# Attention ahead of a gated layer: keys projected one pair of heads earlier, and two steps taken off TensorE

## The chip, the cores and the metric

The kernel runs on one core of one Trainium2 chip. The metric is the time of one execution in device microseconds; several executions are timed and their median is compared. A profiled execution has a span, from its first to its last instruction, and its own time, which is a little longer.

## The reference

What is computed, in short:

```python
batch, n_heads, seq, head_dim, n_features = 8, 8, 576, 64, 128

def phi(x):                                   # x: q or k, times 64 ** -0.25
    h = x @ omega.T - sum(x * x) / 2          # [.., seq, 128]
    return exp(h - max(h)) / sqrt(128)        # max over the 128 features of a token

q_p, k_p = phi(q_s), phi(k_s)
kv  = einsum('bhsm,bhsd->bhmd', k_p, v)
z   = k_p.sum(axis=2)                         # over the 576 tokens
num = einsum('bhsm,bhmd->bhsd', q_p, kv)
den = einsum('bhsm,bhm->bhs', q_p, z)[..., None] + 1e-06
x   = (num / den).transpose(0, 2, 1, 3).reshape(4608, 512)

out = ((x @ w_a) * (x @ w_b)) @ w_out         # 512 -> 1536 -> 512, float32
```

## The kernel before, in words

**Two parts.** The attention is done in 32 *pairs*: pair u = 4·b + hp holds heads 2·hp and 2·hp + 1 of batch b. The gated layer is done in *blocks* of the 512 first tokens of a batch (blocks 0 to 7), and block 8 takes the last 64 tokens of all batches. Blocks 0 and 1 multiply straight (`moe_block`: `pa`, `pb`, `o`); from block 2 on two blocks' halves are combined into seven products (sums of x: `Sa`, `Sb`; sums of weights: `t`, `bq`, which travel through DRAM; products `p`, their sums `c`; the product of both sides, `ghl`, times `wo`). Every fp32 product of the layer is three matmuls on a high and a low part, so each x, weight and product passes a CAST (mostly on ACT) and a subtraction (on DVE). While block b runs, the four pairs of batch b + 1 run between its matmuls.

**A pair.** `pair(u)` does the following, tiles named by u's batch and pair:

- `four` projects four chunks of 128 tokens at once, k on rows 0:64 of the array and q on rows 64:128 (`ppk`, `ppq`), copies them to `hk` and `hq`, and takes the maximum (DVE), the bias `sm`, and the exponential (ACT). Main chunks come twice, the last tokens of all four pairs of a batch once (`ht`).
- **z.** POOL adds the nine chunks of `hk` down to two rows of 128 features for each partition (`zs`). ACT and DVE split it into `zr`, and two matmuls with a matrix of ones sum it over the partitions and spread the sum to all of them: `pz`, copied by ACT to `zb`.
- **kv.** Ten matmuls sum k over the tokens (`pkv`, features along the free axis); ACT copies it (`k2`), PE transposes it (`pk`, with `ident`), ACT copies that (`kl`).
- **Division.** Ten DVE operations take each token's denominator (`dn`, from `hq` and `zb`), ACT scales the nine chunks of `hq` by its reciprocal.
- **Turn of q.** One DVE operation transposes `hq` by 32×32 blocks (`qd`); SP stores it to DRAM in four transfers (`qdr`) and loads it back over `hq`, features along the partitions. Pair 7 (`TURN`) and the pairs of batch 0 use nine transposes on PE instead (`pq`).
- **num.** `pm` = `kl` times the turned q; ACT and DVE make x's high and low part of it. The matmuls of `pm` wait in the list `pending` until the next pair's `pkv` takes them along; those of pairs 7 and 31 are issued by themselves.

Pairs 0 to 3 go another way (`tok_tail`).

**What sets the order.** All operations are recorded in a graph, with a planned cost for each engine, a priority, and a *margin*: planned nanoseconds that an operation stays behind the end of its inputs. `Graph.schedule` then walks over planned time and takes, over all engines, the operation that can start first; that is the order of each engine's instructions. A transfer is planned as its bytes at 330 per ns, one transfer behind another, plus 2000 ns:

```python
    def schedule(self, bw=330.0, dma_lat=2000):
...
                begin = max(s, dma_free)
                dma_free = begin + o.bytes / bw
                o.end = dma_free + dma_lat
```

Buffers come in rings of a given number of slots; an operation that needs a new one is placed when the slot's last user is done. SP issues nearly all transfers, in one queue; a transfer that waits for its data holds up those behind it. The first operation of a pair is kept behind a step of the block that runs (`GATES`, four numbers for the four pairs of a batch).

Of the kernel before, what the change touches and what calls it, by code (L numbers as in the profile page):

```python
# [17 lines left out]
P = 128  # L18
# [6 lines left out]
SM = 512  # L25
# [30 lines left out]
class Graph:  # L56
# [3 lines left out]
    def __init__(self):  # L60
        self.ops, self.rings, self.slots = [], {}, {}
# [172 lines left out]
def tile_attention_moe(ctx: ExitStack, tc: tile.TileContext, kqt, kqtt, kqn, kqnt, vx, omst, idn, wab, wout, out):  # L234
# [12 lines left out]
    for name, n in dict(X=2, Xw=0, nat=2, x2=0, v=2, h=CFG["H"], qd=1, kvz=1, sm=3, sq=3, ht=2, Xt=1, xl=0, xts=2, rd=2, x=4, xa=2, xf=2, Sa=2, Sb=2, st=0,  # L247
                        w=NF, u=NF, t=0, tst=0, wo=3, raw=2, a=2, c=0, bq=0, ghl=2, osb=0, ot=0, owr=0, og=0, ogf=0, oc=0, zs=1, z2=1, zb=1, k2=1, kl=2, dn=1, tails=1, zr=1,
# [6 lines left out]
    LATE = dict(wo=["h0", "h1"], ot=["X0", "X1", "h2", "qd0"], owr=["raw0", "raw1"], og=["nat0", "nat1", "ht0", "ht1"], ogf=["xf0", "xf1"],  # L255
# [34 lines left out]
    ones = fixed([P, P], F32R, "ones")  # L290
    junk = fixed([P, M], mybir.dt.bfloat16, "junk")
# [15 lines left out]
    g.op({"ACT": act(M)}, lambda e: nc.scalar.activation(ones.ap[:], om.ap[:], AF.Copy, scale=0.0, bias=1.0), r=[(om, None)], w=[(ones, None)], prio=3000)  # L307
# [134 lines left out]
    def four(nm, b, pri, x, xdep, dst, c0, sm, sq, al, deps, mg, more):  # L442
# [41 lines left out]
        for w in range(2):  # L484
            for c in some:
                g.op({"ACT": 392}, lambda e, c=c, w=w: nc.scalar.activation(  # L486
                    dst[w].ap[:, c], src[w](c), AF.Exp, scale=SC, bias=sm.ap[:, 2, w, c:c + 1]),
                    r=[(held[w][0] if len(held[w]) == 1 else (dst[w], c)), (sm, (c0, w))], w=[(dst[w], c)], prio=pri + 3 + w)
# [5 lines left out]
    def pair(u, gate):  # L494
# [59 lines left out]
        def zadd(eng, n, o, a, c, r, w, al=()):  # L554
            g.op({"POOL": pool2(n)}, lambda e: ENG[e].tensor_tensor(o(), a(), c(), op=ALU.add), r=r, w=w, alloc=list(al), prio=pri)  # L555
# [12 lines left out]
        g.op({"DVE": dve(2 * M)}, subber(lo, lambda: flat(zs), hi), r=[(zs, None), (zr, 0)], w=[(zr, 1)], prio=pri + 9)
        pz = g.buf("at", [P, 2 * M], F32, f"pz{nm}", more)

        def broadcast(e):
            nc.tensor.matmul(pz.ap[:], ones.ap[:], hi(), start=True, stop=False)
            nc.tensor.matmul(pz.ap[:], ones.ap[:], lo(), start=False, stop=True)
        g.op({"PE": mm(2, 2 * M)}, broadcast,
             r=[(zr, None), (ones, None)], w=[(pz, None)], alloc=[pz, zb], prio=pri + 10, margin=mg and mg + CFG["SUMS"])
        g.op({"ACT": act(2 * M)}, copier(lambda: zb.ap.rearrange("p j m -> p (j m)"), lambda: pz.ap[:]), r=[(pz, None)], w=[(zb, None)], prio=pri + 10)
# [19 lines left out]
        pk = g.buf("at", [P, 2, D], F32, f"pk{nm}", more)  # L596
        kl = g.buf("kl", [P, 2, D], F32, f"kl{nm}")
        g.op({"PE": 108}, lambda e: nc.tensor.transpose(pk.ap.rearrange("p j d -> p (j d)"), k2.ap[:], ident.ap[:]), r=[(k2, None), (ident, None)],
             w=[(pk, None)], alloc=[pk, kl], prio=pri + 5, margin=mg)
# [630 lines left out]
```

## Time and profile before

| | |
|---|---|
| runs shown (us) | 1075.25, 1071.83, 1072.91; median 1072.91 |
| profiled execution: own time, span | 1071.77, 1070.0 |
| granted TensorE clock | 1.00 |
| busy: PE, PE's weight loads, DVE, ACT, POOL | 1053.8, 928.8, 867.2, 591.1, 106.4 |
| idle time of PE | 16.2 |
| DMA | 305.61 MB in all, 286 GB/s; queue 1 (SP's) 303.55 MB, 82.8% of 16 engines' span |
| the chain that ended last | PE 82%, DVE 7%, ACT 5%, DMA 3% |

Times are in microseconds. Matmuls are pipelined, and an instruction's duration in the profile reaches into the next one's; from the start of one to the start of the next is shorter than the duration. A group of instructions has an engine, the tiles it writes and reads (`pz<-zr,ones`), a shape, a count, the busy time and the mean of one, and the engine's idle time just ahead of it with what ended most of it.

### The profile page before, as it was taken

How to read it: one execution, taken by the hardware profiler on the slowest of the kernel's cores; microseconds unless marked ns; L12 is line 12 of the kernel's file. 1: busy time of each engine (PE TensorE's matmuls, PEld its weight loads, DVE VectorE, ACT ScalarE, POOL GpSimd, SP SyncE). 2: the span in 40 equal slices, each digit the busy share in tenths (PEclk: the TensorE clock that was granted, in tenths of full speed). 3: DMA queues.
4: the chain of work that ended last, by engine and by line, in shares of the span. 5: the costliest groups of instructions: out<-in, count | busy, mean ns of one | idle time of the engine just before them, and what ended most of it. 6: DMA issues, size and time to landing. Idle time of an engine off the chain costs nothing.

```text
span 1070.0 us, 22015 instructions
## 1 busy us (share of the span) xinstructions
PE 1053.8 (98%) x7899; PEld 928.8 (87%) x7899; DVE 867.2 (81%) x2145; ACT 591.1 (55%) x1599; POOL 106.4 (10%) x176
## 2 busy tenths in 40 slices
PE   9999999999999999999999999999999999999997
PEld 7878777868788889888888988888888989999997
DVE  6999986989886788777886879778876777998766
ACT  7997767666764646554645566464645423333111
POOL 0021111111110101010111111010101000000000
PEclk9999999999999999999999999999999999999999
DMA  9877966797898888978888888988796799999991
GB/s 359 306 240 230 335 198 208 243 377 274 283 320 295 276 301 269 339 264 289 295 312 295 273 298 270 332 265 299 257 323 196 261 334 304 319 336 344 352 305 50
DMA packets 118270, 305.61 MB, mean 286 GB/s; under 512 B 16656, under 2 KB 35856, under 8 KB 118160
## 3 DMA queue, kind: packets, MB, share of 16 engines
q1 hardware_dynamic: 117296, 303.55, 82.8%
q8 instruction: 62, 1.02, 0.4%
q10 hardware_dynamic: 864, 0.66, 0.2%
q14 instruction: 48, 0.39, 0.1%
HBM read 249.43 MB, written 54.72 MB: 284 GB/s over the span
## 4 chain that ended last, share of the span: by engine, by line
PE 82%; DVE 7%; ACT 5%; DMA 3%; issue 1%; POOL 1%; SPq 0%; ACTq 0%; DVEq 0%
PE p L1047 34%; PE o L785 19%; PE ppk L452 5%; PE pb L956 5%; PE pa L956 5%; PE o_P L853 4%; PE pkv L588 3%; PE pm L647 2%; DMA td<-ts 1%; DVE c L1057 1%; ACT hq L619 1%; ACT hk L486 1%; DMA out_dram<-osb 1%; PE p L853 1%; PE pn L720 1%
## 5 line engine op out<-in xcount | busy, mean ns | idle before, releaser
L1057 DVE TENSOR_TENSOR c<-p,c 128x512 f32<-128x512 f32 (+1 forms) x336 | 207.7, 618 | 93.0 <-PE p L1047 86.7
L785 PE MATMUL o<-wo,ghl 128*128 128x512 f32 x1008 | 270.6, 397 | 0.3 <-DVE ghl L282 0.3
L785 PEld LDWEIGHTS o<-wo,ghl 128*128 128x128 f32 x1008 | 175.5, 188 | 32.0 <-DVE ghl L282 1.2
L1047 PE MATMUL p<-Sa,t 128*128 128x256 f32 x1008 | 144.6, 281 | 1.6 <-ACT c L274 1.6
L1047 PEld LDWEIGHTS p<-Sa,t 128*128 128x128 f32 x1008 | 133.1, 188 | 7.6 <-ACT c L274 2.4
L555 POOL TENSOR_TENSOR z<-hk 128x256 f32<-128x256 f32 x56 | 45.2, 807 | 690.3 <-ACT hk L486 488.9
L274 ACT COPY c<-p 128x256 f32<-128x256 f32 x84 | 31.1, 371 | 125.9 <-PE p L1047 72.7
L486 ACT ACTIVATE hk<-hk,sm 128x128 f32<-128x128 f32 x192 | 62.3, 392 | 46.7 <-DVE sm L482 38.7
L619 ACT ACTIVATE hq<-hq,dn 128x128 f32<-128x128 f32 x224 | 70.6, 392 | 26.6 <-DVE dn L615 24.9
L956 PE MATMUL pb<-x,wb 128*128 128x512 f32 x288 | 75.2, 401 | 0.0
L956 PE MATMUL pa<-x,wa 128*128 128x512 f32 x288 | 73.7, 398 | 0.9 <-DVE x L282 0.9
L1047 PE MATMUL p<-Sb,t 128*128 128x256 f32 x504 | 74.5, 283 | 0.0
L1047 PE MATMUL p<-Sb,bq 128*128 128x256 f32 x504 | 74.5, 283 | 0.0
L1047 PE MATMUL p<-x,t 128*128 128x256 f32 x504 | 73.7, 282 | 0.7 <-ACT oc L274 0.7
L1047 PEld LDWEIGHTS p<-x,t 128*128 128x128 f32 x504 | 69.1, 188 | 5.9 <-ACT oc L274 1.1
L452 PE MATMUL ppk<-om,X 64*128 64x128 f32 x512 | 73.9, 285 | 0.0
L452 PE MATMUL ppq<-om,X 64*128 64x128 f32 x512 | 73.4, 284 | 0.1
L452 PEld LDWEIGHTS ppk<-om,X 64*128 64x128 f32 x512 | 61.7, 187 | 13.5 <-issue 3.4
L1047 PE MATMUL p<-x,wb 128*128 128x256 f32 x504 | 71.2, 284 | 1.6 <-DVE c L1057 1.5
L609 DVE CUSTOM_DVE_ANT_0 junk<-hq,zb 128x128 bf16<-128x128 f32 x224 | 65.6, 293 | 8.6 <-ACT zb L274 6.5
L1047 PE MATMUL p<-x,wa 128*128 128x256 f32 x504 | 71.2, 286 | 1.0 <-DVE c L1057 0.9
L1047 PEld LDWEIGHTS p<-x,wb 128*128 128x128 f32 x504 | 65.9, 188 | 5.1 <-DVE c L1057 2.0
(185 smaller groups left out, 2027.5 us busy)
## 6 DMA issues: line engine op xcount, KB each, us to landing
t<-td SPq DMA_DIRECT2D x168, 512.0 KB, 5.6
wo<-wod SPq DMA_DIRECT2D x96, 512.0 KB, 5.8
bq<-bd SPq DMA_DIRECT2D x84, 256.0 KB, 5.6
X<-in_kqt_dram SPq DMA_DIRECT2D x31, 512.0 KB, 5.7
qdr<-qd SPq DMA_DIRECT2D x108, 144.0 KB, 4.3
hq<-qdr SPq DMA_DIRECT2D x27, 576.0 KB, 6.5
raw<-in_wab_dram SPq DMA_DIRECT2D x24, 512.0 KB, 6.2
td<-ts SPq DMA_DIRECT2D x24, 512.0 KB, 5.9
```

Source lines behind the costliest of these rows:

```text
L274: nc.scalar.copy(o(), i())
L452: nc.tensor.matmul(pps[w].ap[:, c * M:c * M + M], x()[rows, c * P:c * P + P], om.ap[rows], start=True, stop=True)
L486: g.op({"ACT": 392}, lambda e, c=c, w=w: nc.scalar.activation(dst[w].ap[:, c], src[w](c), AF.Exp, scale=SC, bias=sm.ap[:, 2, w, c:c + 1]), ...
L555: g.op({"POOL": pool2(n)}, lambda e: ENG[e].tensor_tensor(o(), a(), c(), op=ALU.add), r=r, w=w, alloc=list(al), prio=pri)
L588: nc.tensor.matmul(pkv.ap[D * j:D * j + D, 0:M], vb.ap[:, vc, 0:D], c(), start=(n == 0), stop=(n == 4))
L609: g.op({"DVE": 413}, lambda e, c=c, j=j, rr=rr, qc=qc: nc.vector.tensor_tensor_reduce(out=junk.ap[rr], in0=qc(), in1=zb.ap[rr, j], scale=1 ...
L619: g.op({"ACT": 392}, lambda e, c=c, src=src: nc.scalar.activation(hq.ap[:, c], src(), AF.Copy, scale=dn.ap[:, c:c + 1]), r=[sd, (dn, None) ...
L785: nc.tensor.matmul(po.ap[:], ghl.ap[:, gi, t * P:(t + 1) * P], wo.ap[:, wi], start=(n == 0 and i == 0), stop=(n == NF - 1 and i == 2))
L853: nc.tensor.matmul(pb.ap[:, t], A[0](ai)[:, t * P:(t + 1) * P], W[0](wi), start=begin and t == j == 0, stop=stop and t == 1 and j == 2)
L956: nc.tensor.matmul(pb.ap[:], wt.ap[:, wi, c], xs[c].at(xi), start=(c == 0 and i == 0), stop=(c == NC4 - 1 and i == 2))
L1047: nc.tensor.matmul(pb.ap[:, half], wcol(wi, c), xc(xi, c), start=n == 0, stop=n == 5)
L1057: g.op({"DVE": dve(n)}, lambda e: nc.vector.tensor_tensor(c4.ap[:, o], pb.ap[:, half], y(), op=ALU.add), r=[*((pb, k) for k in range(half. ...
```

## The change

From pair 4 on, `shifted` takes the place of `pair`. It changes these things:

1. **k runs a pair ahead of q.** `first_k` does the k side of pair 4 by itself. Then step u projects the k chunks of pair u + 1 together with the q chunks of pair u, so the number of projection groups is the same; the host lays the k chunks out anew. The ring `h` of three buffers becomes `hk` (one, eight chunks) and `hq` (two, ten chunks). The first pair of the next batch is now recorded ahead of every block, before only of blocks 2 to 6.
2. **z without PE.** POOL's adds stay. DVE transposes the two rows of 128 by 32×32 blocks, sums each block to one number per partition (`zq`), ACT brings the four groups of 32 partitions together (three small copies), DVE sums and transposes them (`zw`, `zx`). SP stores `zx` (1 KB, `zdr`) and loads it back to all partitions (`zb`, 128 KB). `zr`, `ones`, `pz` go.
3. **kv within q's transfers.** `k2` is transposed by DVE as a tenth chunk of `qd`, so the four stores have 160 KB instead of 144 and the load 640 instead of 576; ACT copies `kl` out of the loaded `hq`. `pk` goes. Pair 7 goes this way too, so its nine `pq` go.
4. **num two steps behind kv.** `pkv` of pair u + 1 takes along `pm` of pair u − 1. The last two `pm` are issued by themselves.
5. **Margins.** Behind the landings of `zb`, of the loaded `hq` and ahead of the first division and of `kl` there are planned margins that differ for batch 1, batch 2 and later ones (`ZD`, `ZB`, `BACK2`, `HQ`; `BACK` was 1500).

The core of the diff:

```diff
-CFG = dict(TW=(), ..., H=3, TURN=(7,), BACK=1500, ...)
+CFG = dict(ZS=800, ZB=(1500, 3000, 5000), ZD=(1500, 3000, 4500), HQ=(2500, 4000, 5000), BACK2=(1500, 2500, 4000), TW=(), ...)
...
-    for name, n in dict(X=2, ..., h=CFG["H"], qd=1, kvz=1, ..., ht=2, ..., zs=1, z2=1, zb=1, k2=1, kl=2, dn=1, tails=1, zr=1,
+    for name, n in dict(X=2, ..., hk=1, hq=2, qd=1, kvz=0, ..., ht=3, ..., zs=1, z2=1, zb=2, k2=2, kl=1, dn=1, tails=0, zq=2, zx=2,
...
+    def shifted(u, gate):
...
+            xb = load("X", [P, 8 * P], f"X{nm}", lambda: kqt[b, hp], early)
...
+                lead = [four(nm, b, pr + 10 * i, ..., [(hk, 0), (hq, 0)], 4 * i, sm, sq, ...)]
+            zbs[u + 1] = z_sums(u + 1, pr, hk, mg)
...
+            k2s[u + 1] = kv_burst(u + 1, pr + 40, hk, vb, 500)
...
+        divide(u, pr, hq, zbs[u])
+        qT = turn(u, pr, hq, k2s[u])
+        num(u, pr, hq, qT)
...
+    def mar(u, name):
+
+        return CFG[name][min(u // NHP, 3) - 1]
...
-        def broadcast(e):
-            nc.tensor.matmul(pz.ap[:], ones.ap[:], hi(), start=True, stop=False)
-            nc.tensor.matmul(pz.ap[:], ones.ap[:], lo(), start=False, stop=True)
...
+        def groups(e):
+            nc.vector.transpose(flat(z2), flat(zs))
+            nc.vector.tensor_reduce(zq.ap[:, 0], flat(z2).rearrange("p (c r) -> p c r", r=32), axis=X, op=ALU.add)
+        g.op({"DVE": 2 * dve(2 * M)}, groups, r=[(zs, None)], w=[(z2, None), (zq, 0)], alloc=[zq], prio=pri, margin=CFG["ZS"])
...
+            for i in range(1, 4):
+                nc.scalar.copy(zq.ap[0:32, i], zq.ap[32 * i:32 * i + 32, 0])
...
+            nc.vector.tensor_reduce(zw.ap[0:32, 0:8], zq.ap[0:32, 0:4].rearrange("p i c -> p c i"), axis=X, op=ALU.add)
+            nc.vector.transpose(zx.ap[0:32], zw.ap[0:32])
...
+        g.op({"SP": 330}, dma(lambda: zd, lambda: zx.ap[0:8]), ..., nbytes=32 * 8 * 4)
+        zload.append(g.op({"SP": 330}, dma(lambda: flat(zb), lambda: zd.rearrange("c r -> (c r)").partition_broadcast(P)), ..., margin=mar(u, "ZD")))
...
-        g.op({"PE": 108}, lambda e: nc.tensor.transpose(pk.ap.rearrange("p j d -> p (j d)"), k2.ap[:], ident.ap[:]), r=[(k2, None), (ident, None)],
-             w=[(pk, None)], alloc=[pk, kl], prio=pri + 5, margin=mg)
-        g.op({"ACT": act(2 * D)}, copier(lambda: kl.ap[:], lambda: pk.ap[:]), r=[(pk, None)], w=[(kl, None)], prio=pri)
...
+        g.op({"DVE": dve(M)}, lambda e: nc.vector.transpose(qd.ap[:, :, NCH], k2.ap.rearrange("p (j r) -> p j r", r=32)),
+             r=[(k2, None)], w=[(qd, 1)], prio=pr + 110)
...
+        g.op({"ACT": act(M)}, copier(lambda: kl.ap[:], lambda: view()[:, :, NCH]), r=[(hq, None)], w=[(kl, None)], alloc=[kl], prio=pr + 120, margin=mar(u, "HQ"))
...
-        ahead = 1 < b and b + 1 < B
-        if ahead:
+        if b + 1 < B:
             attention(b + 1, [0])
```

How this moves instructions is shown at three places. In the rows a tile's number behind its name tells one buffer's use from another; `x_3_3` is x of block 3 from its last pair, `t3_...` weights' sums of block 3.

**PE, where batch 4 begins.** Before, from the `pm` of pair 15 (`pm_3_3`, taken along by `pkv_4_0`) past `pz` and `pk` of pair 16:

```order
L647 MATMUL pm_3_3_4972<-hq_3_3_4323,kl_3_3_4744 64x512 x2
L649 MATMUL pkv_4_0_4970<-hq_3_3_4323,kl_3_3_4744 64x64 x2
L1047 MATMUL p1_3610<-x_2_2_3267,wb10_1679 128x256 x3
L1047 MATMUL p1_3610<-x_2_3_3563,wb10_1679 128x256 x3
L1047 MATMUL p1_3610<-Sa_2_0_3311,t2_510_4655 128x256 x3
L1047 MATMUL p1_3610<-Sa_2_1_3606,t2_510_4655 128x256 x3
L572 MATMUL pz_4_0_5017<-zr_4_0_4991,ones_68 128x256
L573 MATMUL pz_4_0_5017<-zr_4_0_4991,ones_68 128x256
L1047 MATMUL p0_3609<-Sa_2_0_3311,t2_510_4655 128x256 x3
L1047 MATMUL p0_3609<-Sa_2_1_3606,t2_510_4655 128x256 x3
L598 MATMUL pk_4_0_5030<-ident_66,k2_4_0_4971 128x128
```

Now, from the `pkv` of pair 17 on, which takes the same `pm_3_3` along:

```order
L696 MATMUL pkv_4_1_5169<-hk_4_1_4781,v_4_0_4453 64x128 x8
L696 MATMUL pkv_4_1_5169<-htk4_4567,v_4_0_4453 64x128 x2
L764 MATMUL pm_3_3_5171<-hq_3_3_4469,kl15_5156 64x512 x2
L766 MATMUL pkv_4_1_5169<-hq_3_3_4469,kl15_5156 64x64 x2
L903 MATMUL o2_1_4095<-wo2_8_4907,ghl2_8_5005 128x512 x3
L903 MATMUL o2_2_4125<-wo2_8_4907,ghl2_8_5005 128x512 x3
L903 MATMUL o2_3_4134<-wo2_8_4907,ghl2_8_5005 128x512 x3
L1165 MATMUL p1_3771<-x_3_2_4707,wa0_580 128x256 x3
L1165 MATMUL p1_3771<-x_3_3_5172,wa0_580 128x256 x3
```

No `pz` and no `pk` are left, and the first matmul that reads `x_3_3` stands 12 matmuls behind the burst with `pm_3_3`; before, 34 rows lay between them (one row is often three matmuls).

**ACT, at the same place.** Before, from the split of z to the copy of `pk`:

```order
L274 CAST zr_4_0_4991<-zs_4_0_4826 128x256
L274 CAST x_3_3_4973<-pm_3_3_4972 128x512
L274 COPY xts3_4103<-pkv_4_0_4970 128x64
L274 COPY k2_4_0_4971<-pkv_4_0_4970 128x128
L274 COPY zb_4_0_5018<-pz_4_0_5017 128x256
L274 CAST Sa_3_0_5033<-st_3_0_4716 128x2x256
L274 CAST Sa_3_1_5045<-st_3_1_5003 128x2x256
L274 COPY kl_4_0_5031<-pk_4_0_5030 128x128
```

Now, around the copy `kl15` out of the loaded `hq_3_3`:

```order
L725 ACTIVATE hq_4_0_4782<-hq_4_0_4782,dn_4_0_5043 128x128 x5
L275 CAST Sb_3_0_5151<-st_3_0_4741 128x2x256
L275 COPY kl15_5156<-hq_3_3_4469 128x128
L725 ACTIVATE hq_4_0_4782<-htq4_4568,dn_4_0_5043 128x128
L275 COPY c3_00_5187<-p0_3770 128x256
L275 CAST ghl2_11_5191<-c2_51_5096 128x512
L275 CAST x_3_3_5172<-pm_3_3_5171 128x512
```

The copies of z are gone from it; `kl` now waits for a transfer instead of PE, and copies of a product (`c3_00`) and the cast of `ghl2_11` stand behind it.

**DVE, in block 0, where weights are converted.** Before, the sixth pair of weights (`wa5`, `wb5`) ahead of the fourth sum of block 0 (`a0_3`):

```order
L276 CAST wa5_1140<-raw15_804 128x512
L276 CAST wb5_1149<-raw16_817 128x512
L282 TENSOR_TENSOR wa5_1140<-raw15_804,wa5_1140 128x512
L282 TENSOR_TENSOR wb5_1149<-raw16_817,wb5_1149 128x512
L329 SCALAR_TENSOR_TENSOR raw17_853<-raw17_853 128x512
L439 TENSOR_REDUCE sq_1_2_1179<-natk_1_2_966 128x8
L964 TENSOR_TENSOR a0_3_1098<-pb0_3_1130,a0_3_1098 128x512
```

Now, from the fifth sum (`a0_4`) on:

```order
L1082 TENSOR_TENSOR a0_4_1274<-pb0_4_1307,a0_4_1274 128x512
L665 STREAM_TRANSPOSE z2_1_2_1239<-zs_1_2_1240 128x256
L666 TENSOR_REDUCE zq_1_2_1353<-z2_1_2_1239 128x8
L715 ISA zero_69,dn_1_1_1295<-hq_1_1_1128,zb_1_1_1196 128x128
L715 ISA dn_1_1_1295 128x1
L283 TENSOR_TENSOR ghl0_4_1356<-a0_4_1274,ghl0_4_1356 128x512
L715 ISA zero_69,dn_1_1_1295<-hq_1_1_1128,zb_1_1_1196 128x128
L715 ISA dn_1_1_1295 128x1
L675 TENSOR_REDUCE zw_70<-zq_1_2_1353 32x8
L676 STREAM_TRANSPOSE zx_1_2_1377<-zw_70 32x32
```

The cast of `wb5` and its subtraction come six and nine rows behind the last one shown, behind the rest of pair 5's division: the four DVE operations of z and pair 5's denominators (`dn_1_1`) now stand ahead of it.

More of the change, by code (lines that the diff above doesn't have):

```diff
@@ L119, in place @@
             best = None
-            for s in [*ring["slots"], *b.more]:
+            for s in [*ring["slots"], *(x for x in b.more if x not in self.hold or self.hold[x].end is not None)]:
                 if any(s == y for _, y in got):
@@ L530, in pair @@
         sm = g.buf("sm", [P, 3, 2, 8], F32, f"sm{nm}")
-        h = [g.buf("h", [P, NCH if b else 8, M], F32, f"h{'kq'[w]}{nm}", CFG["HROOM"] if b == 0 else []) for w in range(2)]
+        h = [g.buf("h" + "kq"[w], [P, NCH if b and w else 8, M], F32, f"h{'kq'[w]}{nm}", CFG["HROOM"] if b == 0 else []) for w in range(2)]
         lead = []
@@ L540, in pair @@
                 ends[b] = [g.buf("ht", [P, NHP, M], F32, f"ht{'kq'[w]}{nm}") for w in range(2)]
-                lead = [four(f"e{nm}", b, pr + 5, lambda: xe.ap[:], [(xe, None)], ends[b], 0, sme, sqe, [*ends[b], sme], [*gate, *lead], mg, more)]
-        he = ends[b]
+                lead = [four(f"e{nm}", b, pr + 5, lambda: xe.ap[:], [(xe, None)], [(t, 0) for t in ends[b]], 0, sme, sqe, [*ends[b], sme],
+                             [*gate, *lead], mg, more)]
         if hp == 0:
             xstage[b] = g.buf("xts", [P, NHP, TL], F32, f"xts{b}")
-        if fast:
-            return tok_tail(b, hp, nm, pr, mg, more, vb, h, xt)
@@ L547, in pair, with first_k @@
-        hk = h[0]
+        tok_tail(b, hp, nm, pr, mg, more, vb, h, xt)
+    def first_k(gate):
+        u, mg = KS, CFG["MARGIN"]
+        b, hp = divmod(u, NHP)
+        nm, pr = f"_{b}_{hp}", 1000 * u
+        early = pr - 1400
+        xe = load("Xt", [P, NHP * P], f"Xe{nm}", lambda: kqtt[b], early)
+        xb = load("X", [P, 4 * P], f"Xk{nm}", lambda: kqt[B - 1, NHP - 1][:, 0:4 * P], early)
+        sqe = natural([("e", kqnt[b], [2, NHP, D])], f"e{nm}", pr, b)
+        sq = natural([("k", kqn[b, hp, 0], [8, D])], f"k{nm}", pr, b)
+        vb = load("v", [P, NCH + 1, VW], f"v{nm}", lambda: vx[b, hp], early + 3)
+        hk = g.buf("hk", [P, 8, M], F32, f"hk{nm}")
+        sm = g.buf("sm", [P, 3, 2, 4], F32, f"smk{nm}")
+        lead = [four(f"k{nm}", b, pr, lambda: xb.ap[:], [(xb, None)], [(hk, 0), (hk, 4)], 0, sm, sq, [hk, sm], gate, mg, [])]
+        last_chunks(b, pr + 5, xe, sqe, [*gate, *lead], mg)
+        zbs[u] = z_sums(u, pr, hk, mg)
+        k2s[u] = kv_burst(u, pr + 40, hk, vb, mg)
@@ new lines, in load, with natural @@
+    def load(ring, shape, name, src, prio):
+        t = g.buf(ring, shape, F32, name)
+        n = 4
+        for k in shape:
+            n *= k
+        g.op({"SP": 330}, dma(lambda: t.ap[:], src), w=[(t, None)], alloc=[t], prio=prio, nbytes=n)
+        return t
+    def natural(srcs, nm, pr, b):
+        tiles = [load("nat", [P, *shape], f"nat{k}{nm}", lambda src=src: src, pr - 1400 + i + 1) for i, (k, src, shape) in enumerate(srcs)]
+        sq = g.buf("sq", [P, 2, 8 // (3 - len(srcs))], F32, f"sq{nm}")
+        if len(srcs) == 1:
+            square_sums([(tiles[0], lambda: sq.ap.rearrange("p w c -> p (w c)"), None)], sq, 8, nm, pr, b, True)
+        else:
+            square_sums([(tiles[w], lambda w=w: sq.ap[:, w], w) for w in range(2)], sq, 8, nm, pr, b, True)
+        return sq
@@ L571, in broadcast @@
-        def broadcast(e):
[L572 to L576, printed above, removed]
+        zq, zx = g.buf("zq", [P, 4, 8], F32, f"zq{nm}"), g.buf("zx", [P, 32], F32, f"zx{nm}")
@@ new lines, in z_sums, with kv_burst @@
+        zload.append(g.op({"SP": 330}, dma(lambda: flat(zb), lambda: zd.rearrange("c r -> (c r)").partition_broadcast(P)), r=[(zd_b, None)], w=[(zb, None)],
+             alloc=[zb], prio=-30, nbytes=P * 2 * M * 4, margin=mar(u, "ZD")))
+        return zb
+    def kv_burst(u, pri, hk, vb, mg):
+        b, hp = divmod(u, NHP)
+        nm, he = f"_{b}_{hp}", ends[b]
+        heads = kv_chunks(hk, hp, he[0])
+        front = pending.pop() if pending else None
+        pkv = g.buf("at", [P, M + TL], F32, f"pkv{nm}")
@@ L1157, in tile_attention_moe @@
         if b + 1 < B:
-            attention(b + 1, range(int(ahead), NHP))
+            attention(b + 1, range(1, NHP))
     flush(100 * len(steps))
```

200 lines of the change are left out of this document (128 added, 72 removed).

## The prediction

> **What bounds the kernel now.** I read the page's busy row, then the table of stretches, then the list of what PE waited for, and at last the order of single PE instructions around those that go.
>
> The page's busy row: engine, busy us, share of the span, instructions.
>
> ```profile
> PE 1053.8 (98%) x7899; PEld 928.8 (87%) x7899; DVE 867.2 (81%) x2145; ACT 591.1 (55%) x1599; POOL 106.4 (10%) x176
> ```
>
> PE leaves 1070.0 − 1053.8 = 16.2 us of its span. The stretches show where the others are close behind it.
>
> ```profile
> core 0: us, PE busy (x) PEld busy (x) DVE busy (x) ACT busy (x) POOL busy (x), PEclk, DMA share, GB/s
> 40.00:140.00 100.00, 98.67 (x572) 77.68 (x571) 98.51 (x233) 84.69 (x205) 15.62 (x20) 1.00 0.75 257
> 140.00:310.00 170.00, 167.84 (x1021) 131.50 (x1019) 145.40 (x384) 116.80 (x311) 24.81 (x38) 1.00 0.80 271
> 540.00:660.00 120.00, 119.35 (x942) 106.85 (x941) 94.13 (x248) 68.82 (x198) 15.89 (x27) 1.00 0.86 291
> ```
>
> From 540 to 660, a stretch about as long as a block, PE is busy 99% of the time at a granted clock of 1.00 and DVE 78%. From 40 to 140, where the weights are converted, DVE is as full as PE (98.5). The waits of PE, with total, count and longest:
>
> ```profile
> PE p L1047 <- DVE c L1057: 2.4, 4, 1.5
> PE pz L572 <- ACT k L274: 1.6, 1, 1.6
> PE pm L647 <- ACT hq L619: 0.7, 1, 0.7
> PE pk L598 <- ACT hk L486: 0.3, 1, 0.3
> ...
> DVE c L1057 <- PE p L1047: 86.7, 106, 2.2
> ```
>
> No row of PE's list names a DMA, and DVE waits 86.7 us for PE where PE waits 2.4 us for DVE. So a PE instruction that goes is worth what it holds up the next one, as long as nothing new makes PE wait.
>
> **What leaves PE.** Three stretches of PE's timeline, around a `pz`, a `pk` and six of the `pq` (start and duration in us; the count is last):
>
> ```profile
> 840.21 0.89 PE L1047 MATMUL p<-Sa,t 128*128 128x256 f32 x6
> 840.93 0.28 PE L572 MATMUL pz<-zr,ones 128*128 128x256 f32 x1
> 841.05 0.28 PE L573 MATMUL pz<-zr,ones 128*128 128x256 f32 x1
> 841.17 0.86 PE L785 MATMUL o<-wo,ghl 128*128 128x512 f32 x3
> ...
> 851.99 0.86 PE L1047 MATMUL p<-Sa,t 128*128 128x256 f32 x6
> 852.69 0.27 PE L598 MATMUL pk<-ident,k 128*128 128x128 f32 x1
> 852.72 0.95 PE L1047 MATMUL p<-Sb,t 128*128 128x256 f32 x6
> 853.50 0.86 PE L785 MATMUL o<-wo,ghl 128*128 128x512 f32 x3
> ...
> 166.51 0.82 PE L686 MATMUL pq<-ident,hq 128*128 128x128 f32 x6
> 167.09 0.95 PE L785 MATMUL o<-wo,ghl 128*128 128x512 f32 x3
> ```
>
> - The sum over tokens (`pz`, two matmuls a pair): from 840.93 to 841.17 are 0.24 us before the next work starts, against durations of 0.28 each. 28 pairs × 0.24 = **6.7 us**.
> - The transpose of kv (`pk`): the next six start 0.03 later, and need 853.50 − 852.72 = 0.78 where the six before needed 0.70. 0.03 + 0.08 = 0.11; × 28 = **3.1 us**.
> - The nine transposes `pq` of pair 7: six hold the next work up for 167.09 − 166.51 = 0.58, and by 0.08 more as behind `pk`: 0.11 each, × 9 = **1.0 us**.
> - The waits of `pz` (1.6) and `pk` (0.3) go with them: **1.9 us**.
>
> The other PE work is the same in number: 28 pairs still have two projection groups each (the first k alone and the last q alone are one group each), 28 kv sums and 28 `pm`; two `pm` run by themselves before and after.
>
> For the transpose a page of the Trainium skill speaks for a larger sum: TensorE: Matmul & The Clock Gate, Part 4: PE-mode transpose, gives about 275 ns in a kernel's context. The trace agrees with that as a duration (0.27), but the next matmul starts 0.03 later; by the page's figure the 28 would be 7.7 us instead of 3.1, and the result 4.6 us lower. I take the starts, since the next work begins by them.
>
> **What comes on the other engines.** The rows with the nearest prices (groups by shape: busy, mean ns):
>
> ```profile
> L627 DVE STREAM_TRANSPOSE qd<-hq 128x1152 f32<-128x1152 f32 x27 | 37.0, 1370 | 2.2 <-ACT hq L619 2.2
> L439 DVE TENSOR_REDUCE sq<-natk 128x8 f32<-128x512 f32 x31 | 20.9, 673 | 0.2
> L282 DVE TENSOR_TENSOR zr<-zs,zr 128x256 fp32r<-128x256 f32 x28 | 11.7, 416 | 8.4 <-ACT zr L274 8.4
> L481 DVE SCALAR_TENSOR_TENSOR sm<-sm,sq 128x8 f32<-128x8 f32 x62 | 10.0, 161 | 0.9
> L274 ACT CAST zr<-zs 128x256 fp32r<-128x256 f32 x28 | 11.4, 406 | 15.2 <-POOL zs L555 15.0
> L274 ACT COPY zb<-pz 128x256 f32<-128x256 f32 x28 | 10.5, 374 | 33.4 <-PE pz L573 33.3
> L274 ACT COPY xts<-pkv 128x64 f32<-128x64 f32 x26 | 5.8, 221 | 0.0
> ```
>
> DVE, each pair: the transpose of 256 columns lies between 256/1152 of 1370 = 0.30 and the 0.42 of an operation as wide; I take 0.40. The reduction of 256 to 8: between half of 0.67 and 0.67; 0.42, as the 256 wide row. The two small ones 0.16 each by the row of 8 elements. The transpose of kv (128 columns): 0.15 to 0.42; 0.25. Together 1.39, and 0.42 of `zr` goes: +1.0 us a pair (0.7 to 1.4), 28 us in all, which makes 867 into 895 (84% of the span). In the stretch 540 to 660 four pairs add 4 to 94 of 120: hidden in DVE's 25 us of waiting for PE. ACT loses 0.41 + 0.37, and gains three small copies (0.22 each at most by `xts`): about nothing, and it is 55% busy. POOL's adds stay.
>
> Where DVE has no room is 40 to 140. Four sums of z come into it, and a part of the k work of one more pair: +4 us and about 1 to 2 us. Against that, its conversions ran far ahead there:
>
> ```profile
> 81.63 0.68 DVE L282 TENSOR_TENSOR wb<-raw,wb 128x512 fp32r<-128x512 f32 x1
> 83.43 0.68 DVE L964 TENSOR_TENSOR a<-pb,a 128x512 f32<-128x512 f32 x1
> ...
> 96.82 2.80 PE pb L956 x12
> ```
>
> Two rows of DVE's timeline and one of the chain: the sixth `wb` is done at 82.3, right ahead of `a0_3` at 83.4, and PE uses it from 96.8: 14 us of lead. In the order of the change it stands behind `a0_4`, so the lead is what pays; what is put off finds room in 140 to 310, where DVE has 170 − 145 = 25 us free. Behind `a0_4` come, by the rows, some 4.4 us of DVE's work up to that `wb`, while PE has 27 matmuls of 512 columns ahead of its use, at 0.23 each 6.3 us. Bounds: nothing if such margins hold, and the whole 6 us as waits of PE if they don't. I take 1 us, nearer to the lower end, since that margin is positive by 2 us.
>
> DMA, with KB and median us to landing, and the one queue's own wait for such a landing (total, times, longest):
>
> ```profile
> qdr<-qd SPq DMA_DIRECT2D x108, 144.0 KB, 4.3
> hq<-qdr SPq DMA_DIRECT2D x27, 576.0 KB, 6.5
> xtd<-xts SPq DMA_DIRECT2D x8, 128.0 KB, 4.6
> q1 hardware_dynamic: 117296, 303.55, 82.8%
> ...
> SPq L285 <- DMA qdr<-qd: 13.8, 21, 2.7
> DMA to landing us min/median/max: 3.8/6.5/9.0
> ```
>
> Per pair 64 KB more each way for kv, 1 KB of z out and 128 KB in, and a whole round trip for pair 7: 28 × 256 KB + 1.2 MB = 8.5 MB of 303.55, so the queue goes from 82.8% to about 85%. On SP a pair's z brings two issues: the load waits for the 1 KB store, which should land after 2 to 4.6 us like the `xtd` store; issues of weights stand behind it. SP did the same for `qdr` 21 times, at up to 2.7 us, and PE waited for no weight. z is needed a whole pair later, a quarter of a block, so its round trip of some 11 us (4.6 and 6.5) is covered. Kv now returns inside `hq`, and ACT copies it out (`kl`) right ahead of `pm`: what stands behind that copy on ACT, in the order the copies of `c` and the next casts, waits if the landing is late. The planner's room behind the landing (2.5 to 5 us of planned time) is at least the 9.0 − 6.5 = 2.5 us by which the slowest landing exceeded the median. I take nothing for it.
>
> At the border of blocks `pm` of the last pair now stands close ahead of the first matmul that reads its x in blocks 3 and 5: 9 matmuls of 512 columns (0.70 for three), 3 of x and its own small ones, some 2.7 us, by the same count 8 us before. The chain behind it is ACT's cast, then DVE's subtraction:
>
> ```profile
> 404.74 1.03 PE L647 MATMUL pm<-hq,kl 128*64 128x512 f32 x4
> 405.81 0.59 ACT L274 CAST x<-pm 128x512 fp32r<-128x512 f32 x1 [0.83 <-PE pm L647]
> ```
>
> The cast ends 406.4; with DVE's 0.4 and 0.7 behind it x is ready 2.8 us after `pm` starts, and PE gets there after 0.9 + 0.2 + 2.7 = 3.8. It fits by 1 us. I take 1 us in all for such places, 0 to 3.
>
> **Sum**, from the profiled execution's 1071.8 (span 1070.0 and 1.8 around it): 1071.8 − 6.7 − 3.1 − 1.0 − 1.9 + 1 + 1 = 1061.1. The median of the runs shown, 1072.9, lies 1.1 above the profiled one; so I expect **1062 us**, with 1057 (no new wait, and 3 us of the old ones gone too) to 1067 (6 us in 40 to 140) for this case.
>
> **Rivals.**
>
> *DVE becomes the bound of the first two blocks.* For it: 98.5% busy against 98.7, and POOL's adds slow it there (below, one cast of 0.41 took 0.96 while POOL worked). Against: the lead above. If nothing is deferred, 6 us up to 140 and some of 8 us more up to 310 show on PE: about half of 10.8 is given back, **1068**.
>
> ```profile
> 54.53 1.06 POOL L555 TENSOR_TENSOR z<-hk 128x256 f32<-128x256 f32 x1 [53.29 <-ACT hk L486]
> 54.92 0.96 DVE L276 CAST wa<-raw 128x512 fp32r<-128x512 f32 x1
> ```
>
> *The time stays.* PE's records overlap, so busy need not mean bound; what goes would leave a gap. Weight loads are in progress in only 87% of the span. Against: in the rows above each group starts the moment that the one ahead allows it, and all of PE's idle time is 16.2 us. **1072**. The Trainium skill has this as a rule (Perfetto Trace Analysis, Identifying the Most-Contended Engine): matmul busy time is no measure, the weight loads' share is. By it PE would have 13% of room; the trace speaks against it, since a 512-column matmul takes 0.23 from start to start (0.70 for three) and a load 0.19.
>
> *ACT's `kl` copies and SP's z loads hold up their queues, and PE behind them: slower.* The place is the copy in front of each `pm`. It gives back the gain if each of 28 costs PE 12.7/28 = 0.45 us; at 0.7, a landing late by 3.2 us behind a room of 2.5, it is 28 × 0.7 − 12.7 = +7: **1080**. For it: waiting copies stand in order on an engine that also feeds `c`. Against: PE waited for `hq` at most 0.7 in all with less room.
>
> **Chances.** 0.72 for 1062; 0.14 for DVE (1068, three quarters of it still more than 0.3% faster); 0.06 for no change; 0.08 for slower. 0.3%, or 3.2 us, is about what a measurement can tell here. Faster: 0.72 + 0.10 = 0.82; within: 0.04 + 0.06 = 0.10; slower: 0.08. The range 1057 to 1071 leaves out the slower case, most of the unchanged one and a little below.
>
> **What would show it.** Right: no `pz` or `pk`, PE some 12 us less in busy or idle, evenly 0.4 a pair, the chain still PE throughout; DVE about 895. Wrong: in 40 to 310 new PE waits for `wa`, `wb` or `ghl` (first rival); rows PE `pm` <- ACT `kl`, or ACT `kl` <- DMA `hq` with many counts, or PE `p` <- DMA `t` (third); a PE idle that grows by what its busy time lost (second).

## The result, and the profile after

The changed kernel takes 1065.95 us (median of six, 1065.04 to 1066.72) where the kernel before takes 1073.49: a ratio of 0.9928 with a 95% interval of 0.9911 to 0.9945, or 7.5 us less. The forecast was 1062, in a range of 1057 to 1071: the direction and the range hold, the gain is 7.5 of the 10.9 forecast.

The profiled execution has a span of 1064.7 us, 5.3 less than before; the profiled one of before was 1.7 below its median, this one is 0.6 above. Its busy row:

```profile
PE 1045.8 (98%) x7806; PEld 920.4 (86%) x7806; DVE 892.0 (84%) x2233; ACT 599.1 (56%) x1646; POOL 107.5 (10%) x177
```

PE is busy 8.0 us less, and its idle time grew from 16.2 to 18.9. DVE has 892.0 against the 895 forecast, and the DMA queue 8.55 MB more at 86.3%:

```profile
q1 hardware_dynamic: 122640, 312.10, 86.3%
```

The same three stretches as before (columns: PE, weight loads, DVE, ACT, POOL busy, then clock):

```profile
40.00:140.00 100.00, 98.01 (x589) 77.28 (x588) 97.68 (x243) 86.30 (x223) 17.11 (x24) 1.00 0.77 247
140.00:310.00 170.00, 167.33 (x996) 131.30 (x995) 157.17 (x420) 124.53 (x336) 29.66 (x42) 1.00 0.88 297
540.00:660.00 120.00, 119.59 (x943) 106.39 (x941) 100.53 (x262) 70.96 (x205) 16.81 (x29) 1.00 0.90 308
```

From 540 to 660 nothing new holds PE up. From 140 to 310 DVE went from 145.4 to 157.2 of 170, and PE is busy 0.5 us less there. What PE waited for (total, times, longest):

```profile
PE p L1165 <- DVE c L1175: 3.4, 5, 1.3
PE ppk L454 <- ACT k L275: 2.1, 2, 1.4
PE p L971 <- issue: 1.7, 1, 1.7
...
PE pb L1074 <- ACT xts L275: 0.6, 1, 0.6
PE pb L1074 <- DVE wb L283: 0.5, 1, 0.5
```

`pz` and `pk` are gone with their 1.9 us. Two new rows count. The projections (`ppk`) wait for ACT's copy `k` out of `pkv`: the two PSUM buffers of the ring `at` hold `pm` and `pkv`, and the projections need both. And one product waits 1.7 us at 901, for a reason that stands one engine further back.

To see where the time went I took, for each matmul, the distance to the next one's start, less the median distance for matmuls of its kind in that trace, and added that up. The medians alone (the work) fall by 10.2 us, which is nearly the 10.8 of `pz`, `pk` and `pq`. What is lost beyond them goes from 23.9 to 29.0 in the first 320 us, from 2.4 to 5.2 between 880 and 920, and falls by 3.4 in the rest. So the forecast gain came, and some 8 us were given back in two places.

**The first place, blocks 0 and 1.** At 181 ACT reaches the three copies that empty `pm` and `pkv` (cast of x, `xts`, `k`) late: a copy of `osb` and three scalings of `hq`, which wait for DVE's `dn`, stand in front (start, duration; idle time before in brackets; the first row's wait is for `dn` as well):

```profile
180.67 0.58 ACT L275 COPY osb<-o 128x512 f32<-128x512 f32 x1 [2.36 <-DVE dn L720]
180.70 0.21 DVE L721 RECIPROCAL dn<-dn 128x9 f32<-128x9 f32 x1
...
181.15 0.98 ACT L725 ACTIVATE hq<-hq,dn 128x128 f32<-128x128 f32 x3
...
182.04 0.57 ACT L275 CAST x<-pm 128x512 fp32r<-128x512 f32 x1
182.50 0.22 ACT L275 COPY xts<-pkv 128x64 f32<-128x64 f32 x1
182.61 0.28 ACT L275 COPY k<-pkv 128x128 f32<-128x128 f32 x1
...
182.94 0.48 PE L454 MATMUL ppk<-om,X 64*128 64x128 f32 x2 [1.40 <-ACT k L275]
```

**The second place, 900 to 908.** ACT waits for a landing, the last of the four loads that bring block 8's x back (`xl`), with the cast of `ghl` behind it:

```profile
ACT x L275 <- DMA xl<-xtd: 3.1, 1, 3.1
```

```profile
896.72 0.37 ACT L275 COPY c<-p 128x256 f32<-128x256 f32 x1 [2.26 <-DVE c L1175]
900.22 0.62 ACT L275 CAST x<-xl 128x512 fp32r<-128x512 f32 x1 [3.13 <-DMA xl<-xtd]
900.75 0.92 ACT L275 CAST ghl<-c 128x512 fp32r<-128x512 f32 x2
```

PE stands still for 1.7 us, and then TensorE's granted clock falls (the seventh number behind the stretch, after POOL's):

```profile
900.00:904.00 4.00, 2.32 (x19) 2.13 (x18) 2.63 (x8) 2.00 (x5) 0.00 (x0) 0.98 0.88 316
904.00:908.00 4.00, 4.00 (x23) 4.00 (x23) 3.32 (x9) 1.41 (x4) 0.00 (x0) 0.59 0.71 196
```

From 904 to 908 PE is busy throughout; at a clock of 0.59 it does 0.41 × 4 = 1.6 us less work. So the wait costs about twice what the list of waits shows.

### The profile page after: what moved, and what is told of

It reads as the page before. It is cut to its first block, busy times and chain, and to the rows that moved or that the text cites. A ratio compares the mean times of both kernels' runs of the same rounds, so it can differ in the third digit from the quotient of the medians.

```text
span 1064.7 us, 22028 instructions
## 1 busy us (share of the span) xinstructions
PE 1045.8 (98%) x7806; PEld 920.4 (86%) x7806; DVE 892.0 (84%) x2233; ACT 599.1 (56%) x1646; POOL 107.5 (10%) x177
## 3 DMA queue, kind: packets, MB, share of 16 engines
q1 hardware_dynamic: 122640, 312.10, 86.3%
## 4 chain that ended last, share of the span: by engine, by line
PE 77%; DVE 13%; DMA 4%; ACT 3%; issue 2%; SPq 0%; ACTq 0%; DVEq 0%
PE p L1165 37%; PE o L903 18%; PE ppk L454 5%; PE o_P L971 4%; PE pa L1074 3%; PE pb L1074 2%; PE pkv L696 2%; PE pm L764 2%; DVE zero L715 1%; DVE c L1175 1%; DVE sm L477 1%; DMA td<-ts 1%; DMA out_dram<-osb 1%; PE pn L838 1%; DVE ghl L283 1%
## 5 line engine op out<-in xcount | busy, mean ns | idle before, releaser
L1165 PE MATMUL p<-Sa,t 128*128 128x256 f32 x1008 | 141.4, 281 | 0.0
L715 DVE CUSTOM_DVE_ANT_0 zero<-hq,zb 128x128 bf16<-128x128 f32 x224 | 75.0, 335 | 2.9 <-ACT c L275 0.2
L1074 PE MATMUL pb<-x,wb 128*128 128x512 f32 x288 | 73.0, 398 | 1.2 <-ACT xts L275 0.6
L490 ACT ACTIVATE hk<-hk,sm 128x128 f32<-128x128 f32 x184 | 59.3, 393 | 23.0 <-DVE sm L485 22.9
```

The costliest lines, as they stand in the source:

```text
L490: g.op({"ACT": 392}, lambda e, c=c, w=w, to=to, at=at: nc.scalar.activation(to.ap[:, at + c], src[w](c), AF.Exp, scale=SC, bias=sm.ap[:, 2 ...
L715: g.op({"DVE": 413}, lambda e, c=c, j=j, rr=rr, qc=qc: nc.vector.tensor_tensor_reduce(out=junk.ap[rr], in0=qc(), in1=zb.ap[rr, j], scale=1 ...
L1074: nc.tensor.matmul(pb.ap[:], wt.ap[:, wi, c], xs[c].at(xi), start=(c == 0 and i == 0), stop=(c == NC4 - 1 and i == 2))
L1165: nc.tensor.matmul(pb.ap[:, half], wcol(wi, c), xc(xi, c), start=n == 0, stop=n == 5)
```

## The experiments

Each was timed beside the kernel before. Where a kernel is set against the changed one, it is by these ratios (changed: 0.9928), and the intervals of both count: each reaches 1 to 2.5 us to either side.

**1 and 2. What the two steps cost PE, in the kernel before.** Each is issued twice, with the order kept.

```diff
+            for _ in range(2):
+                nc.tensor.matmul(pz.ap[:], ones.ap[:], hi(), start=True, stop=False)
+                nc.tensor.matmul(pz.ap[:], ones.ap[:], lo(), start=False, stop=True)
```

> The kernel before, with the two matmuls of each pz issued twice (the second pair writes the same sums again); plan and order as before. My theory, that PE is the bound and such a matmul costs its distance from start to start: 28 x 0.24 = 6.7 us slower than before. Rival, the time is set elsewhere and PE's busy time overlaps: no change (within 1.5 us). Rival, it costs its whole duration of 0.28 each: 28 x 0.56 = 15.7 us slower.

Measured: 1.0059 (1.0044 to 1.0074), 6.3 us slower, with 4.7 to 7.9 in the interval. The price from start to start (6.7) holds; both rivals fall.

```diff
-lambda e: nc.tensor.transpose(pk..., k2.ap[:], ident.ap[:])
+lambda e: [nc.tensor.transpose(pk..., k2.ap[:], ident.ap[:]) for _ in range(2)]
```

> The kernel before, with each transpose pk issued twice into the same buffer; plan and order as before. My theory: 28 x 0.11 = 3.1 us slower. Rival, by the duration of 0.27 each: 7.6 us slower. Rival, PE does not set the time: no change.

Measured: 1.0017 (1.0006 to 1.0027), 1.8 us slower, 0.6 to 2.9. It is less than 3.1, and far from 7.6: a transposition among other matmuls costs much less than its duration.

**3. z back on PE in the changed kernel.**

```diff
+ZPE = lambda u: True
...
+        if ZPE(u):
+            zr = g.buf("zr", [P, 2, 2 * M], F32R, f"zr{nm}", ["ht0", "ht1", "ht2"])
...
+            pz = g.buf("at", [P, 2 * M], F32, f"pz{nm}")
...
+            return zb
+
         zq, zx = g.buf("zq", [P, 4, 8], F32, f"zq{nm}"), g.buf("zx", [P, 32], F32, f"zx{nm}")
```

> The changed kernel (1066.0) with z summed and spread by PE again: zr, ones and pz as before, no DVE sums, no trip of zx and zb through DRAM; k stays a pair ahead, kv stays within q's transfers. My theory: 6.7 us come back on PE, and about 2 us of what block 0 and 1 lost (PE waits for buffers that ACT empties late there) go with DVE's lighter load: 1070 to 1071. Rival, the gain of the change is that of the shift and not of the work taken off PE: no slower than 1067. Rival, the DVE sums cost the first blocks as much as they spare PE elsewhere: 1066 or faster.

Measured: 1071.95 us, 0.9979 (0.9969 to 0.9990). z's way around PE is worth 5.5 us of the gain, half a microsecond more than my theory allowed: the first 320 us do lose 5 less (24.2 by the same count), but four projections at block borders now wait 0.5 to 1.1 each.

**4. kv back on PE in the changed kernel.**

```diff
-        n = NCH + 1
+        n = NCH
...
+        pk = g.buf("at", [P, 2, D], F32, f"pk{nm}")
+        kl = g.buf("kl", [P, 2, D], F32, f"kl{nm}")
```

> The changed kernel (1066.0) with kv transposed on PE again (pk, with its copy kl), q's transfers back to 144 and 576 KB; k a pair ahead and z by DVE and DMA stay; pair 7 still turns by DVE. My theory: 3.1 us come back on PE, less 0 to 1 for DVE's lighter load: 1068 to 1069. Rival, the landing that kl waits for costs more than the transpose: 1065 or faster.

Measured: 1073.52 us, 0.9994 (0.9982 to 1.0005): 7 us worse than the changed kernel where I expected 3. Between the two profiled executions it is 5.2, of which the medians (the work) make 2.2, and longer distances between starts 3.2. The waits:

```profile
PE ppk L454 <- ACT hk L275: 2.5, 3, 1.1
PE p L1167 <- DVE c L1177: 2.1, 4, 0.8
PE pm L766 <- DMA hq<-qdr: 1.7, 2, 1.0
PE ppq L454 <- DVE x L283: 1.3, 2, 1.1
PE pk L706 <- ACT hk L490: 1.3, 2, 1.1
```

The projections and `pk` itself wait here; `pk` takes one of the two PSUM buffers between `pkv` and the next projections. I read these waits as that contention, which no run took away by itself. The row of `pm` is another matter: there PE waits for the loaded `hq`, as it never did in the changed kernel.

**5. The shift alone.** Both edits of 3 and 4 together.

> The changed kernel with both z and kv on PE again (zr, ones, pz, pk, kl as before), so that of the change only the shift is left: k a pair ahead of q, kv two pairs ahead of num, pair 7 turned by DVE, the room behind q's landing. My theory now: the two steps on PE are worth 6.3 and 1.8 us by themselves (both issued twice), yet each put back costs 5.5 and 7: the difference is that pz and pk also hold the two PSUM buffers that the projections, pkv and pm use, and that the shift has made scarce. Then the shift alone is slower than the kernel before: 1076 to 1079 against 1074. Rival, the parts add and the shift is neutral but for pair 7: 1073 to 1074. Rival, the shift brings a gain of its own: under 1071.

Measured: 1079.01 us, 1.0045 (1.0031 to 1.0059), 4.8 us slower than before. The shift, which I had costed at nothing, costs: it spares 1.4 us of work (pair 7's `pq`), and loses 7.8 us more in the distances between starts. The list of waits says where a part of it is lost:

```profile
PE pz L673 <- DVE x L285: 2.6, 3, 1.3
PE ppk L458 <- ACT hk L277: 2.5, 3, 1.0
```

`pz` doesn't read x, and a projection doesn't read `hk`. DVE's subtraction for x is what empties the buffer of `pm`, and ACT's copy to `hk` what empties that of the projections before: both rows are waits for one of the two PSUM buffers. With the changed kernel's two steps taken off PE, `pz` and `pk` are out of PSUM, and the whole is a gain. Two things stay open. "The shift" here is also the new margins, rings and the earlier recording of a batch's first pair; and no run took z and kv off PE without it, so that their DRAM trips need its room is not shown.

**6. Room for the PSUM buffers.**

```diff
-            t = max(t, o.end + self.LAT)
+            t = max(t, o.end + self.LAT + (600 if s[:2] == "at" and o.end < 300000 else 0))
```

> The changed kernel; the planner takes each of the two PSUM buffers of the at ring to come free 600 ns later than it does, for users up to planned 300 us (blocks 0 and 1). All work is the same. My theory, that in blocks 0 and 1 PE waits at the projections for ACT to empty pm and pkv (3.6 us of stretched projections and 3 us of waits): about half of that goes, 1063 to 1064.5. Rival, DVE bounds those blocks, and what PE doesn't wait for there it waits for elsewhere: 1066, within 1. Rival, the later start of pairs delays x: slower, 1068.

Measured: 1072.58 us, 0.9991 (0.9980 to 1.0002), 6.8 us worse than the changed kernel, against all three expectations. On my theory it says nothing, since the edit made longer waits of another kind:

```profile
PE pm L764 <- ACT kl L275: 3.7, 1, 3.7
...
PE pa L1074 <- ACT x L275: 2.3, 1, 2.3
```

Here `kl` is copied late ahead of `pm`, in one place, but not for the reason of the prediction's third rival, a late landing. On ACT it stands right behind the three small copies of `zq`, and these wait for DVE:

```profile
184.03 0.61 ACT L671 COPY zq<-zq 32x8 f32<-32x8 f32 x3 [0.17 <-DVE zq L666]
184.66 0.30 ACT L275 COPY kl<-hq 128x128 f32<-128x128 f32 x1
```

Behind the wait the clock is 0.50 from 183.8 to 197.5, two stretches of which are these:

```profile
186.00:190.00 4.00, 1.68 (x9) 0.69 (x5) 1.01 (x2) 4.00 (x14) 0.00 (x0) 0.50 0.87 319
190.00:194.00 4.00, 3.27 (x19) 2.29 (x18) 1.20 (x3) 1.33 (x3) 0.00 (x0) 0.50 0.72 188
```

**7 and 8. More load on DVE, in the same order**, early (pairs 4 to 11) and late (pairs 16 to 31).

```diff
+            for _ in range(2 if u < 12 else 1):          # 8: if u >= 16
+                nc.vector.transpose(flat(z2), flat(zs))
+                nc.vector.tensor_reduce(zq.ap[:, 0], ...)
```

> The changed kernel, plan and order as they are; the transpose and the reduction of z on DVE are issued twice for pairs 4 to 11 (blocks 0 to 1 mostly), 8 x 0.85 = 6.8 us more on DVE. If DVE's load bounds blocks 0 and 1: 1069 to 1073. If DVE is hidden there as the prediction had it with 1 us of cost: 1066 to 1067.

Measured: 1073.11 us, 0.9990 (0.9981 to 1.0000): 6.8 us more of DVE's work cost 6.7. The waits that were there grew, and a long one again drew the clock down:

```profile
PE ppk L454 <- ACT k L275: 3.9, 2, 2.5
...
188.00:194.00 6.00, 6.00 (x25) 4.53 (x24) 2.95 (x5) 4.62 (x12) 0.00 (x0) 0.50 0.85 277
```

The clock is 0.50 from 187.2 to 194.1, which costs half of 6.8 us, 3.4. By the starts the first 320 us lose 6.0 more than in the changed kernel, so beside the clock some 2.6 us of PE's time go for 6.8 of DVE's; 320 to 880 loses 1.9 more, and 880 to 920 1.4 less. That the price equals the added work is chance. In blocks 0 and 1 DVE's work is not fully covered: a part of it reaches PE by way of ACT's copies.

> The changed kernel, plan and order as they are; the same two DVE instructions issued twice for pairs 16 to 31, 16 x 0.85 = 13.6 us more on DVE where it waits for PE. The prediction's view that DVE's new work is hidden from block 2 on: 1066 to 1067.5. Rival, DVE's work is in the path there too: 1070 or more.

Measured: 1069.35 us, 0.9963 (0.9950 to 0.9977): 13.6 us of DVE's work cost 3.8, between theory and rival. Most is hidden, a quarter isn't; by the distances of starts it lies all over 320 to 880 (25.5 to 29.5 there). Which wait carries it I did not settle.

**9. xl used later.**

```diff
-    ..., w=[xt.part(0)], alloc=list(al), prio=pri, deps=gate)
+    ..., w=[xt.part(0)], alloc=list(al), prio=pri, deps=gate, margin=4000 if b == B else 0)
```

> The changed kernel (1066.0); the first uses of xl, block 8's x loaded back from DRAM, get a planned margin of 4000 ns, so that the cast of the last xl stands later on ACT. In the changed kernel ACT waits 3.1 us for that landing at 897, ahead of the cast of ghl; PE then stands still for 1.7 us, and its granted clock is 0.50 from 904 to 907, some 1.7 us more. My theory: both go, 1062.5 to 1064. Rival, only PE's idle time goes and the clock falls anyway: 1064.3. Rival, what stands behind ghl is late for another reason: 1066.

Measured: 1070.79 us, 0.9971 (0.9956 to 0.9986): worse by 4.6. ACT no longer waits for `xl`, but what stands behind block 8's x in DVE's and ACT's order moved back as well (DVE's first sum of it got the same margin), and PE waited longer, for `ot`:

```profile
903.46 0.54 PE L971 MATMUL o_P<-ot,ghl 128*128 128x256 f32 x1 [2.90 <-ACT ot L275]
```

**10. z on PE for pairs 4 to 11 only**, the edit of 3 under `u < 12` (with one buffer instead of two for `zq` and `zx`, for space).

> The changed kernel with z by zr, ones and pz on PE for pairs 4 to 11 (blocks 0 and 1), by DVE and DMA from pair 12 on. My theory, DVE bounds blocks 0 and 1 (1 us there costs 1 us, as the doubled sums showed): 8 us less on DVE win back the 4 to 5 us that PE loses there, 8 x 0.24 = 1.9 us come on PE: 1062 to 1064. Rival, the waits there come from the two PSUM buffers, of which pz takes one: 1066 to 1069.

Measured: 1067.30 us, 0.9942 (0.9919 to 0.9964): no better, and in the range of the rival. Yet in its place the theory holds and the rival's reason doesn't: the first 320 us lose 24.1 instead of 29.0, as little as before the change, though `pz` takes a PSUM buffer there again. But the 16 matmuls cost 2.1, and from 320 to 880 it loses 3.5 more, mostly at three block borders where `ppk` waits 0.5 to 1.3. Whether the single `zq` and `zx` or only the other order brings those, I did not try.

**11. 9 and 10 together.**

> Both of them: the margin behind xl, and z on PE for pairs 4 to 11. My theory: the gains add, 1059 to 1062. If one of the two theories falls, the other's gain alone.

Measured: 1070.78 us, 0.9971 (0.9958 to 0.9985): as 9 alone. The same wait for `ot` (2.9 us) and the same fall of the clock are in it, and a second fall at 556.

**12. xl loaded earlier.** Since using it later failed, the load gets one more place to go: the third buffer of `ht`, free by then. The last load is issued at 867 instead of 894.

```diff
-    xl = g.buf("xl", [P, SM], F32, f"xl{hp}", ["X0", "X1", "hk0", "hq0", "hq1"])
+    xl = g.buf("xl", [P, SM], F32, f"xl{hp}", ["X0", "X1", "hk0", "hq0", "hq1", "ht2"])
```

> The changed kernel (1066.0); the last of the four loads of xl may also take the third buffer of the ring ht, and is so issued 18 transfers earlier on SP; the order of ACT around it hardly changes (the cast of that xl comes one or two places earlier). My theory: the wait of ACT for that landing (3.1 us at 897) goes, with it PE's 1.7 us at 901 and the 1.7 us that the granted clock of 0.50 costs behind it: 1062 to 1064, with a clock of 1.00 through 900 to 910. Rival, as when the cast was put later: the work behind it stands in another order and PE waits for ot instead: 1068 to 1070. Rival, something else holds ghl: 1066.

Measured: 1063.40 us (1062.81 to 1064.68), 0.9911 (0.9897 to 0.9924). That is 2.5 us below the changed kernel by the medians and 1.8 by the ratios, whose intervals overlap; all five of its runs lie below all six of the other's. It is the fastest kernel of this study. ACT's cast of `ghl` starts 2.3 us earlier and waits for no landing; then PE's busy share and clock where it had stood still:

```profile
898.47 1.07 ACT L275 CAST ghl<-c 128x512 fp32r<-128x512 f32 x2 [2.03 <-DVE c L1214]
...
900.00:904.00 4.00, 3.48 (x30) 3.28 (x29) 4.00 (x10) 1.67 (x4) 0.00 (x0) 1.00 0.75 201
904.00:908.00 4.00, 4.00 (x35) 4.00 (x36) 4.00 (x11) 1.41 (x3) 0.00 (x0) 1.00 0.93 328
```

0.5 us of idle time instead of 1.7, and the clock stays at 1.00. So the landing of `xl` was what stopped PE at 901. What that is worth in time is known less well, since the two intervals overlap.

## Why the prediction was right, point by point

- **PE bounds the kernel, and a matmul that goes is worth its distance from start to start.** Right: 6.7 for `pz` measured as 6.3 (experiment 1) and 5.5 (3), and the sum of medians fell by 10.2 where the prediction took 10.8. `pk` was sized at 3.1 and measures 1.8 by itself. The rival that the time stays is excluded by experiment 1.
- **The work goes in number as it was (costed at 0).** This is the step that failed most in principle: the shift by itself is 4.8 us slower. I counted PE's groups and not the PSUM buffers that they hold. `pm` and `pkv` now fill both buffers just ahead of projections, and `pz` and `pk`, when they are still there, want them too; experiment 5 shows `pz` and the projections waiting for just these. How much of the 4.8 that is stays open, as no run had a third buffer. Since the change takes the two steps away, most of it didn't show in the sum.
- **The crowded stretch, sized at 1 us (0 to 6).** It measures 5.1, by the starts up to 320. The place was right and the mechanism in part: I looked at the weights' conversions, and their wait is only 0.5 (`pb` for `wb`). The larger waits run from DVE by `dn` to ACT and from ACT's copies to the PSUM buffers. DVE's five new operations measure 1.54 us a pair where I took 1.39, and one old row was undersized: the division, which I held unchanged, now runs beside POOL's adds of the next pair.

```profile
L609 DVE CUSTOM_DVE_ANT_0 junk<-hq,zb 128x128 bf16<-128x128 f32 x224 | 65.6, 293 | 8.6 <-ACT zb L274 6.5
```

```profile
L715 DVE CUSTOM_DVE_ANT_0 zero<-hq,zb 128x128 bf16<-128x128 f32 x224 | 75.0, 335 | 2.9 <-ACT c L275 0.2
```

The first is before, the second after: 9.4 us more for the same 224 instructions. By single instructions, 49 of them now lie for more than half beside an add of POOL and take 0.53 in the mean; the 175 that lie beside none take 0.28. Before, only 9 lay beside one. The total of DVE came out near the forecast only because the planner gave casts of `ghl` to ACT, which rose by 8 where I had nothing.
- **Block borders, 1 us (0 to 3).** No row of PE's list names a new wait of a first product for x; 0 by the profile.
- **Landings, costed at 0.** `kl`, `zb` and SP's queue cost nothing that the list of waits shows. But a landing on ACT did cost, `xl`, which the prediction didn't look at: 2.8 by the starts, with the clock, and 1.8 to 2.5 by taking it away (experiment 12). The third rival had the mechanism, a landing that ACT waits for ahead of what PE needs, at the wrong tile.
- **DVE hidden from block 2 on.** Nearly: a quarter of added load shows (experiment 8).

Between the two profiled executions 5.3 us are gained where the sum had 10.7. By the starts: 0.6 less work went than forecast; the first 320 us lost 5.1 more where 0.9 less was forecast (1 for the crowded stretch, less the 1.9 of the old waits, both in it); 2.8 came at 900; and the rest lost 3.4 less where 1 more was forecast for the borders. The last I can't explain; it saved the forecast some 4 us, and that is luck. By the medians the miss is 3.4.

## What to carry to other kernels

Work taken off a bounding engine is worth its distance from start to start, and doubling it in the old order measures that price without moving anything else. When steps are shifted against each other, count the buffers that they hold at the same time and the engine that empties them, not only the instructions: here the shift alone was slower, and the gain came from what was taken off PE along with it. Where ACT waited for a landing, an earlier load helped and a later use only moved the wait on.

## What the runs showed of the hardware

A pause of PE can cost twice: its own length, and a slower clock behind it. In each trace the granted clock changes only at whole multiples of 3.41 us from its other changes (in experiment 6 it falls at 183.84 and again at 910.88, which is 213 × 3.413 later). The slow stretch at 0.50 lasts one such step in most cases, two in experiment 7 and four in experiment 6.

I cut every profiled execution into these steps, without its start and its end, and added up the time that PE stood still in each. At a clock of 1.00 six steps had 1.68 us or more of it (the changed kernel at 901, experiment 6 twice, 7, 9 and 11), and the step behind each had a clock of 0.50. Of all steps with less (the next longest had 1.57), only two were followed by 0.50: those of experiments 3 and 11 near 555, with 1.14 and 1.35. This is the one of experiment 3, with the stretch behind it:

```profile
554.00:558.00 4.00, 2.86 (x26) 2.25 (x24) 1.86 (x5) 1.56 (x3) 0.00 (x0) 1.00 1.04 387
558.00:562.00 4.00, 4.00 (x19) 3.71 (x19) 2.25 (x9) 3.40 (x10) 1.64 (x3) 0.57 0.82 298
```

In both a group of projections follows the pause within the same step. Experiment 10, with 1.29 at the same place and these projections in the next step, had no such fall. Whether the projections are the reason, no run decides.

So the length of a pause alone doesn't tell. The longest without a fall behind it was 1.84 us, in experiment 2; it lies over a border between two steps, with 1.52 in one:

```profile
869.67 1.08 PE L647 MATMUL pm<-hq,kl 128*64 128x512 f32 x4 [1.84 <-DMA hq<-qdr]
...
866.00:870.00 4.00, 2.16 (x13) 1.64 (x14) 0.47 (x1) 0.37 (x1) 0.00 (x0) 1.00 1.06 362
870.00:874.00 4.00, 4.00 (x35) 3.56 (x32) 2.56 (x6) 1.82 (x4) 0.00 (x0) 1.00 0.98 359
```

The place at 901 in experiment 10 had a pause of 1.61 us, 1.21 of it in one step, and kept its clock too:

```profile
900.00:904.00 4.00, 2.39 (x20) 2.20 (x19) 2.64 (x7) 1.45 (x3) 0.00 (x0) 1.00 0.85 313
904.00:908.00 4.00, 4.00 (x35) 4.00 (x34) 4.00 (x11) 1.97 (x5) 0.00 (x0) 1.00 0.77 230
```

The borders lie elsewhere in each execution (the first change comes 4.0 to 6.9 us after the start), so whether a pause of this length costs twice is partly chance.

The Trainium skill (TensorE: Matmul & The Clock Gate, Part 1) tells of a free-running window of about 3.4 us, and of at least one idle window as what throttles. The steps of 3.41 us here agree with such a window; for the idle time in it, half was enough.
